# Seven VectorE operations for nine in the seven-product groups, and two more groups in that form

## The chip, the cores and the metric

The kernel runs on one core of one Trainium2 chip. The metric is device time in microseconds (us) of one execution of the whole program. TensorE does the matmuls, VectorE and ScalarE work on their results, SyncE (SP) issues nearly all transfers. In the rows PE is TensorE, PEld its weight loads, DVE is VectorE, ACT is ScalarE.

## What is computed

An attention over channels, then two feed-forward layers over 6016 tokens of 256 channels with 2048 hidden features each. The weights of the layers come as 64-bit floats and the kernel makes 32-bit ones of them.

```python
def _attn_ref(q, k, v, tau):
    qn = q / (np.linalg.norm(q, axis=1, keepdims=True) + 1e-06)
    kn = k / (np.linalg.norm(k, axis=1, keepdims=True) + 1e-06)
    s = kn.transpose(0, 2, 1) @ qn / tau
    a = softmax(s)                       # over the last axis
    return (v @ a).astype(np.float32)

def _moe_ref(x, w_in, w_out):
    r = np.maximum(x @ w_in, 0.0)
    return ((r * r) @ w_out).astype(np.float32)

def _moe2_ref(x, w_in, w_out):
    h = x @ w_in
    return (np.maximum(0.01 * h, h) @ w_out).astype(np.float32)
...
x = _attn_ref(**attn).reshape(6016, 256)
return _moe2_ref(_moe_ref(x, **moe), **moe2)
```

## The kernel before

**Tiling.** The tokens are cut into six pairs (p = 0 to 5) of two halves. A half has 512 tokens, in pair 4 it has 448. The hidden features are cut into eight groups (g = 0 to 7) of 256. One unit n is one layer, one pair and one group, so there are 96 units, and the last one is n = 95. In a unit the hidden values are a 2 x 2 block of quadrants: two blocks of 128 features (fb) by two halves of tokens.

**Precision.** Each operand is split into a high part, which ScalarE rounds (a cast), and a low part, which VectorE forms by subtracting the high part (`low`, line 109). A product is then three matmuls (`mm3`, line 540, matmul in line 543).

**First matrix product of a unit.** From unit 4 on it takes seven products F1 to F7 instead of eight: the weights w_in and the tokens are combined to sums and differences of quadrants first (`sums`, line 204; `prepare_x`), and the results accumulate in two banks, ha and hb (or hc and he). ScalarE and VectorE take them out into the tiles c, and ScalarE applies the nonlinear function.

**Second matrix product of a unit.** It has two forms. In the plain form ("P") there are eight products, and two double casts and two double low parts (of two quadrants, 1024 columns, each) prepare the operands. In the seven-product form ("S", the groups that the table GROUPS names) the products are P1 to P7. Their operands are quadrants and differences of quadrants, which VectorE forms in place; per unit that is nine operations of VectorE: a double low part G0, low part B22, the differences T1, T3, T2 and T4, a double low part G1, and the low parts T3 and T2. P2, P3, P4 and P7 accumulate in four y banks, P1 and P6 in the bank yA, P5 in yF. P6 of several units (a batch) is kept back and done together at the batch's end. VectorE empties yA into the sums P1 and U (`take_shared`, line 1672).

**The end of a pair.** `combine` adds the sums P1, U and V and the bank yF to the y banks; results are transposed on VectorE and stored.

**The end of the last pair.** The pair (2, 5) is mixed: groups 0 to 4 are in the seven-product form, the rest is plain. `BY_TOKENS` is the first group whose half 1 is done in another way (`second_by_tokens`, line 577): the tokens are the stationary operand, so that the result needs no transpose, in 24 matmuls of 256 columns per group into four banks (`by_token`). Before, these are groups 6 and 7. What the seven-product groups summed for half 1 must then join in: `combine_last` (line 1802) adds U, V and yF to the y banks on VectorE, transposes the two sums of half 1 into a tile o, and SP stores this tile to memory (`ys`, line 1834) and loads it back with the tokens in rows (`sums`, line 1841). `finish_last` (line 598) adds the four by-token banks to it and stores the result.

**The order.** A planner in the kernel (`build`, `simulate`) places tasks on the engines from costs and due times and writes each engine's list of instructions in that order. Each engine then takes its list strictly in turn and waits where an operand isn't there. On TensorE the first products F1 to F7 of a unit go in a fixed sequence, with second products of earlier units put between.

Of the kernel before, what the change touches and what calls it, by code (L numbers as in the profile page):

```python
# [19 lines left out]
P = 128  # L20
# [8 lines left out]
def attn_moe_moe2(  # L29
# [22 lines left out]
    GROUPS = {(1, 4): tuple(range(6)), (1, 5): tuple(range(6)), **{(2, p): tuple(range(7)) for p in range(5)}, (2, 5): tuple(range(5))}  # L52
# [43 lines left out]
    wi_d = {(L, g): dram.tile([P, 2, 8, P], F32, name=f"wi{L}_{g}") for L in (1, 2) for g in range(NG)}  # L96
# [27 lines left out]
    class Unit:  # L124
# [6 lines left out]
        def load(self):  # L131
# [6 lines left out]
            nc.sync.dma_start(t.rearrange("p a b w -> p a (b w)"), src)  # L138
# [29 lines left out]
        def into(self):  # L168

            if self.kind == "i" or self.blocks:  # L170
# [5 lines left out]
                return self.x, self.to[:, 0], self.to[:, 1]  # L176
# [21 lines left out]
        def store(self):  # L198
            if self.kind == "o":
                nc.sync.dma_start(wo_d[self.L, self.g], raw(self.to))  # L200
            elif self.L == 2:
                nc.sync.dma_start(wi_d[2, self.g][:, :, 1:], raw(self.to[:, :, 1:]))

    def sums(x, A11=1, A22=2, S1=4, S2=5, S3=6, S4=7):
# [8 lines left out]
    def out_sums(x):  # L213
        return sums(x, A11=2, A22=1, S1=5, S2=6, S3=7, S4=4)
# [355 lines left out]
    def second(n, half, fb, d):  # L570
# [3 lines left out]
        wo = both(wo_t[L, p, g], d, fb)  # L574
        mm3(y, wo, both(g_t[n, half], fb, slice(0, w)), begins((L, p, half, d)))

    def second_by_tokens(n, fb):
# [5 lines left out]
        for t in range(WIDTH[p] // P):  # L583
            if first:
                by_token.append(y_bank(L, p, 1, t) if t < KC else bank("ce"[t - KC], "y"))
            for m, (a, b) in enumerate(((0, 1), (0, 0), (1, 0))):
# [3 lines left out]
                    wo[:, b, :, fb],  # L590
# [44 lines left out]
    def shared(n, product, bank_key, first):  # L635
# [8 lines left out]
        else:  # L644
            a = both(late_w[n, "S2" if product == "P6" else "S3"], 0)
        x = {"P1": lambda: both(g_t[n, "G0"], 0, sl), "P2": lambda: both(g_t[n, "G0"], 1, sl),
             "P3": lambda: both(b_t[n, "B22"], sl), "P4": lambda: both(g_t[n, "G1"], 1, sl),
             "P5": lambda: both(g_t[n, "G1"], 0, sl), "P6": lambda: both(b_t[n, "T2"], sl),
             "P7": lambda: both(b_t[n, "T3"], sl)}[product]()
# [8 lines left out]

    def result(n, half, w, fb=None):
        c = c_t[n, half]  # L660
        return c[:, :, :w] if fb is None else c[:, fb, :w]
# [208 lines left out]
    KEEP = 8  # L870
    LATE_FIRST = True
# [9 lines left out]
    CONV_BEGIN, CONV_END = 1.4, 4  # L881
    N0 = 4
    FOLD_AFTER = "F1"
# [52 lines left out]
    A = {"A11": 1, "A22": 2, "A12": 3, "S1": 4, "S2": 5, "S3": 6, "S4": 7}  # L936
# [23 lines left out]
    FROM = {"P1": "G0", "P2": "G0", "P3": "B22", "P4": "G1", "P5": "G1", "P6": "T2", "P7": "T3"}  # L960
# [26 lines left out]
    def build(base):  # L987
# [33 lines left out]
        def convert(u, due, loaded=None, first=None, pace=4, begin=0):  # L1021
# [14 lines left out]
            if blocks:  # L1036
                raw_ = Buf("whl", 2, d(4))
                t = T("DVE", 3, d(4), u.high, deps=[t], alloc=raw_, uses=[w, cm])
                for i in range(4):
                    t = T("DVE", 1.1, d(4.2 + i / 10), lambda i=i: (sums if u.kind == "i" else out_sums)(u.x)[i](),  # L1040
                          deps=[t], uses=[raw_])
                to = Buf("wis", 1, d(5))
                t = T("ACT", 4.6, d(5), u.round, deps=[t], alloc=to, uses=[raw_])
                t = T("DVE", 5.2, d(6), u.low, deps=[t], uses=[raw_, to])
# [30 lines left out]
        def fold_sums(n, at_):  # L1075
# [19 lines left out]
            for i in range(4):  # L1095
                a = T("DVE", 1.1, at_ + 11 + i, lambda i=i: r["s"][i](), deps=[a], uses=[xb])
            h_ = T("ACT", 4.6, at_ + 16, lambda: nc.scalar.copy(wi_t[1, 0, g][:, 0], r["x"]), deps=[a], uses=[xb, b])
            lo = T("DVE", 5.2, at_ + 22, lambda: low(wi_t[1, 0, g][:, 1], r["x"], wi_t[1, 0, g][:, 0]), deps=[h_], uses=[xb, b])
            wi_ready[1, 0, g] = wi_ready[n + 1] = lo
            stores["i", 1, g, "s"] = T(  # L1100
                "SP", "wi", at_ + 30, lambda: nc.sync.dma_start(wi_d[1, g][:, :, 1:], raw(wi_t[1, 0, g][:, :, 1:])),
# [247 lines left out]
        def load_wi(n):  # L1349
            L, p, g = units[n]  # L1350
            b = wi_b[n] = Buf("wi", 3, base[n - 2] + 0.5)
            if n < 2 * NG and g < N0:
# [11 lines left out]
                def high():  # L1364
                    nc.scalar.copy(r["w"][:, 0, 4:], r["x"][:, 4:])
# [578 lines left out]
```

## Time and profile before

| | us |
|---|---|
| median of 3 runs | 1001.35 (1000.79 to 1002.28) |
| the profiled execution, its own time | 1002.93 |
| its span, first to last instruction | 1001.1 |
| TensorE busy | 994.6 |
| VectorE busy | 901.4 |
| ScalarE busy | 804.4 |

The granted TensorE clock is 1.000 over the whole span. Matmuls overlap in the records, so that a record is longer than the distance to the next one; the distance of starts tells what a matmul takes in a stream. The wait of a matmul for an operand shows as idle time of its weight load (PEld).

### The profile page before, as it was taken

How to read it: one execution, taken by the hardware profiler on the slowest of the kernel's cores; microseconds unless marked ns; L12 is line 12 of the kernel's file. 1: busy time of each engine (PE TensorE's matmuls, PEld its weight loads, DVE VectorE, ACT ScalarE, POOL GpSimd, SP SyncE). 2: the span in 40 equal slices, each digit the busy share in tenths (PEclk: the TensorE clock that was granted, in tenths of full speed). 3: DMA queues.
4: the chain of work that ended last, by engine and by line, in shares of the span. 5: the costliest groups of instructions: out<-in, count | busy, mean ns of one | idle time of the engine just before them, and what ended most of it. 6: DMA issues, size and time to landing. Idle time of an engine off the chain costs nothing.

```text
span 1001.1 us, 13148 instructions
## 1 busy us (share of the span) xinstructions
PE 994.6 (99%) x4528; PEld 837.3 (84%) x4528; DVE 901.4 (90%) x1314; ACT 804.4 (80%) x1184; POOL 0.7 (0%) x6
## 2 busy tenths in 40 slices
PE   9999999999999999999999999999999999999998
PEld 7888888887888888998888888888888888998887
DVE  4899999988988977999999999999999999998985
ACT  6799978877878777888898888779788788887773
POOL 0000000000000000000000000000000000000000
PEclk9999999999999999999999999999999999999999
DMA  9786559788978967965665665666577586676553
GB/s 339 281 253 205 200 193 287 266 308 296 332 284 294 318 249 265 316 219 206 223 209 200 229 215 202 201 217 226 172 219 233 182 239 227 210 233 220 195 143 84
DMA packets 160946, 234.97 MB, mean 235 GB/s; under 512 B 53232, under 2 KB 97264, under 8 KB 158576
## 3 DMA queue, kind: packets, MB, share of 16 engines
q1 hardware_dynamic: 160160, 233.48, 69.0%
q8 instruction: 36, 0.59, 0.2%
q10 hardware_dynamic: 720, 0.66, 0.2%
q14 instruction: 30, 0.25, 0.1%
HBM read 187.70 MB, written 46.40 MB: 234 GB/s over the span
## 4 chain that ended last, share of the span: by engine, by line
PE 97%; DMA 2%; DVE 0%; ACT 0%; ACTq 0%; issue 0%; SPq 0%
PE y L543 37%; PE ha L543 21%; PE hb L543 16%; PE yA L543 7%; PE yF L543 3%; PE hc L543 3%; PE sT L386 3%; PE he L543 2%; PE h L704 2%; PE pw L252 1%; DMA qk<-in_k_dram 1%; DMA qk<-in_q_dram 1%; PE y L587 0%; DVE o L552 0%; ACT e L472 0%; ACTq L338 0%
## 5 line engine op out<-in xcount | busy, mean ns | idle before, releaser
L543 PE MATMUL y<-g,wo 128*128 128x512 f32 (+1 forms) x1344 | 350.5, 387 | 0.0
L543 PEld LDWEIGHTS y<-g,wo 128*128 128x128 f32 x1344 | 252.1, 188 | 49.5 <-DVE wo L110 0.4
L543 PE MATMUL ha<-x,wi 128*128 128x512 f32 (+1 forms) x960 | 265.6, 385 | 0.0
L110 DVE TENSOR_TENSOR g<-c,g 128x1024 fp32r<-128x1024 f32 (+1 forms) x192 | 228.0, 1197 | 18.7 <-ACT g L674 13.9
L543 PEld LDWEIGHTS ha<-x,wi 128*128 128x128 f32 x960 | 180.0, 188 | 33.8 <-ACT c L1504 0.7
L543 PE MATMUL hb<-x,wi 128*128 128x512 f32 (+1 forms) x720 | 199.6, 386 | 0.1
L543 PEld LDWEIGHTS hb<-x,wi 128*128 128x128 f32 x720 | 134.3, 188 | 26.2 <-DVE c L550 1.7
L1612 DVE TENSOR_TENSOR c<-c 128x512 f32<-128x512 f32 (+1 forms) x208 | 139.9, 672 | 7.1 <-ACT c L691 1.2
L1587 ACT CAST g<-c 128x1024 fp32r<-128x1024 f32 (+1 forms) x104 | 105.2, 1023 | 5.1 <-PE y L543 2.4
L110 DVE TENSOR_TENSOR b<-c,b 128x512 fp32r<-128x512 f32 (+1 forms) x156 | 102.5, 668 | 2.0 <-ACT b L1605 1.7
L1605 ACT CAST b<-c 128x512 fp32r<-128x512 f32 (+1 forms) x156 | 93.1, 608 | 10.5 <-DVE c L1612 4.7
L681 ACT ACTIVATE c<-c 128x1024 f32<-128x1024 f32 (+1 forms) x96 | 100.0, 1043 | 1.5
L674 ACT CAST g<-c 128x1024 fp32r<-128x1024 f32 (+1 forms) x88 | 91.7, 1044 | 1.6
L1504 ACT COPY w<-ha 128x512 f32<-128x512 f32 (+1 forms) x80 | 46.2, 577 | 49.9 <-PE ha L543 49.6
L691 ACT ACTIVATE c<-c 128x512 f32<-128x512 f32 (+1 forms) x98 | 60.7, 621 | 8.8 <-DVE c L552 8.5
L1504 ACT COPY u<-ha 128x512 f32<-128x512 f32 (+1 forms) x80 | 46.0, 575 | 9.8 <-PE ha L543 6.9
L110 DVE TENSOR_TENSOR x<-xr,x 128x1024 fp32r<-128x1024 f32 (+3 forms) x47 | 49.1, 1051 | 0.6 <-ACT x L1261 0.6
L386 PE MATMUL sT<-qk 128*128 128x256 f32 x188 | 42.1, 382 | 1.4 <-DMA qk<-in_k_dram 1.3
L543 PE MATMUL yA<-g,wo 128*128 128x512 f32 (+1 forms) x156 | 42.9, 383 | 0.0
L543 PE MATMUL yF<-g,ws 128*128 128x512 f32 (+1 forms) x156 | 42.9, 383 | 0.0
L543 PE MATMUL y<-b,ws 128*128 128x512 f32 (+1 forms) x156 | 42.9, 383 | 0.0
L543 PE MATMUL y<-b,wo 128*128 128x512 f32 (+1 forms) x156 | 42.8, 383 | 0.0
(137 smaller groups left out, 1202.4 us busy)
## 6 DMA issues: line engine op xcount, KB each, us to landing
wi<-wi SPq DMA_DIRECT2D x88, 896.0 KB, 5.6
wo<-wo SPq DMA_DIRECT2D x84, 512.0 KB, 4.5
ws<-wo SPq DMA_DIRECT2D x120, 128.0 KB, 4.0
wst<-in_moe_w_in_dram SPq DMA_DIRECT2D x16, 512.0 KB, 6.0
wst<-in_moe_w_out_dram SPq DMA_DIRECT2D x16, 512.0 KB, 6.8
wi<-wis SPq DMA_DIRECT2D x8, 896.0 KB, 6.1
wo<-wis SPq DMA_DIRECT2D x7, 1024.0 KB, 7.6
wo<-wos SPq DMA_DIRECT2D x13, 512.0 KB, 5.8
```

The costliest lines, as they stand in the source:

```text
L110: tt(lo, x, raw(hi), op=ALU.subtract)
L252: nc.tensor.matmul(pw[:, i * 2 * P : (i + 1) * 2 * P], eT[:, a, j, i * P : (i + 1) * P], whl[g][:, b, j], start=t == 0 and (i == 0 or g == 0),
L386: nc.tensor.matmul(sT[j][:, :C], t[:, 0, i, j * P : (j + 1) * P], t[:, 1, i], start=n == 0 and i == 0, stop=last_tile and i == g - 1,)
L543: nc.tensor.matmul(ps, a[m], b[n], start=first and i == 0, stop=i == 2, skip_group_check=True)
L674: nc.scalar.copy(g_t[n, half][:, 0, :, :w], c)
L681: nc.scalar.activation(c, c, AF.Square)
L691: nc.scalar.activation(c, c, AF.Prelu, alpha=0.01)
L704: nc.tensor.matmul(h_t[n, half, fb][:, :w], a[i], b[j], start=start, stop=stop, skip_group_check=True)
L1504: nc.scalar.copy(to, h(0))
L1587: nc.scalar.copy(g_t[n, name][:, 0, :, :w], result(n, half, w))
L1605: nc.scalar.copy(b_t[n, name][:, 0, :w], c(half, fb))
L1612: tt(c(*to), c(*a), c(*b), op=ALU.subtract)
```

## The change

- **Seven operations for nine.** In seven-product units the tiles c hold a feature block's two halves together (by row) instead of a half's two feature blocks. The operands pair up in another way: GA is a row of results as it stands (for P2 and P3), GB is the other row after one difference T3 (for P1 and P7), GC is the first row with T2 subtracted from both quadrants in one operation (for P5 and P4), and T2 is a sum in a small tile of its own (t2, one buffer). VectorE has three double low parts, T3, T2, the double subtraction and one single low part. ScalarE has three double casts and a single one instead of two and three.
- **Two more groups.** Pair 5 of the first layer has seven groups in the form instead of six, pair 5 of the second layer has six instead of five. `BY_TOKENS` follows from that: it becomes 7, so that group 6 of the last pair is plain in both halves and only group 7 goes by tokens.
- **Weights.** The sum S4 is written over the quadrant A21, which isn't used any more, so that the tile wi has seven quadrants instead of eight and is stored and loaded in one piece. Two of the four operations on the sums become one double subtraction; for the second weights of the seven-product groups that asks for the two halves in turned places (`turned`), so each of these loads becomes two.
- **Planner.** The conversion of the second layer's weights may begin at 1.2 pairs instead of 1.4 (`CONV_BEGIN`), and the folding of the attention into the weights stands behind F2 instead of F1 (`FOLD_AFTER`). In a unit that doesn't end a batch, P1 stands behind P2 and P3.

```diff
-    GROUPS = {(1, 4): tuple(range(6)), (1, 5): tuple(range(6)), **{(2, p): tuple(range(7)) for p in range(5)}, (2, 5): tuple(range(5))}
+    GROUPS = {(1, 4): tuple(range(6)), (1, 5): tuple(range(7)), **{(2, p): tuple(range(7)) for p in range(5)}, (2, 5): tuple(range(6))}
     BY_TOKENS = max(GROUPS.get((2, 5), (-2,))) + 2
...
-        wi_t[key] = wpool.tile([P, 2, 8, P], F32R, tag="wi", name="wi", bufs=3)
+        wi_t[key] = wpool.tile([P, 2, 7, P], F32R, tag="wi", name="wi", bufs=3)
...
-            nc.sync.dma_start(t.rearrange("p a b w -> p a (b w)"), src)
+            to = t.rearrange("p a b w -> p a (b w)")
+            if turned(self.kind, self.L, g):
+                for b in range(2):
+                    nc.sync.dma_start(to[:, 1 - b], src[:, b])
+            else:
+                nc.sync.dma_start(to, src)
...
+        S2 = S3 + 1
         return [
             lambda: tt(x[:, S1], x[:, 0], x[:, A22], op=ALU.add),
-            lambda: tt(x[:, S3], x[:, A11], x[:, 0], op=ALU.subtract),
-            lambda: tt(x[:, S2], x[:, S1], x[:, A11], op=ALU.subtract),
+            lambda: tt(two(S3, S2), two(A11, S1), two(0, A11), op=ALU.subtract),
             lambda: tt(x[:, S4], x[:, 3], x[:, S2], op=ALU.subtract),
         ]
...
-    CONV_BEGIN, CONV_END = 1.4, 4
+    CONV_BEGIN, CONV_END = 1.2, 4
     N0 = 4
-    FOLD_AFTER = "F1"
+    FOLD_AFTER = "F2"
...
-    FROM = {"P1": "G0", "P2": "G0", "P3": "B22", "P4": "G1", "P5": "G1", "P6": "T2", "P7": "T3"}
+    FROM = {"P1": "GB", "P2": "GA", "P3": "GA", "P4": "GC", "P5": "GC", "P6": "T2", "P7": "GB"}
+    PART = {"P1": 0, "P2": 0, "P3": 1, "P4": 0, "P5": 1, "P7": 1}
...
-            t1 = T("DVE", 3 * s, t0 + 59, sub, (0, 0), (1, 0), (0, 0), deps=[n22, g0], uses=cb)
-            t3 = T("DVE", 3 * s, t0 + 61, sub, (1, 0), (1, 1), (1, 0), deps=[n12, t1], uses=cb[1:])
-            t2 = T("DVE", 3 * s, t0 + 65, sub, (1, 1), (1, 1), (0, 0), deps=[t3, b22], uses=cb)
-            t4 = T("DVE", 3 * s, t0 + 67, sub, (0, 1), (0, 1), (1, 1), deps=[t2], uses=cb)
...
+            def t3():
+                c = result(n, 1, w)
+                tt(c[:, 1], result(n, 0, w)[:, 1], c[:, 1], op=ALU.subtract)
+
+            def t2():
+                c = result(n, 1, w)
+                s_t[n, "t2"] = tpool.tile([P, 1, 512], F32, tag="t2", name="t2", bufs=T2_BUFS)
+                tt(s_t[n, "t2"][:, 0, :w], c[:, 0], c[:, 1], op=ALU.add)
+
+            def t4_t1():
+                c = result(n, 0, w)
+                tt(c, c, s_t[n, "t2"][:, :, :w].to_broadcast([P, 2, w]), op=ALU.subtract)
...
+            ca, cbb = cb[1], cb[0]
+            b = g_b[n, "GA"] = Buf("g", 4, t0 + 45)
+            t = T("ACT", A2, t0 + 45, pair_cast, "GA", 0, deps=[n22, n21], alloc=b, uses=[ca])
+            low_of[n, "GA"] = ga = T("DVE", D2, t0 + 52, pair_low, "GA", 0, deps=[t], uses=[b, ca])
+            d3 = T("DVE", 3 * s, t0 + 50, t3, deps=[n22, n12, n11], uses=cb)
+            b = g_b[n, "GB"] = Buf("g", 4, t0 + 52)
+            t = T("ACT", A2, t0 + 52, pair_cast, "GB", 1, deps=[d3], alloc=b, uses=[cbb])
+            low_of[n, "GB"] = gb = T("DVE", D2, t0 + 58, pair_low, "GB", 1, deps=[t], uses=[b, cbb])
+            t2b = Buf("t2", T2_BUFS, t0 + 53)
+            d2 = T("DVE", 3 * s, t0 + 53, t2, deps=[d3], alloc=t2b, uses=[cbb])
+            d41 = T("DVE", D2, t0 + 54, t4_t1, deps=[ga, d2], uses=[ca, t2b])
...
-                own = own if ends else [p1, *own]
+                own = own if ends else [*own, p1]
```

**How the order moves at the end of TensorE's list.** ha and hb are the last unit's first products, yA takes P1 and P6, yF takes P5, y stands for the four y banks and the by-token banks (the last row of each). These are the last twelve rows before the program's end. Before:

```order
L543 MATMUL yA<-b,ws 128x512 x3
L543 MATMUL y<-g,wo 128x512 x3
L543 MATMUL hb<-x_7811,wi 128x512 x3
L543 MATMUL ha<-x_7916,wi 128x512 x3
L543 MATMUL y<-g,wo 128x512 x3
L543 MATMUL hb<-x_7854,wi 128x512 x3
L543 MATMUL ha<-x_7854,wi 128x512 x3
L543 MATMUL y<-g,wo 128x512 x6
L543 MATMUL ha<-x_7916,wi 128x512 x3
L543 MATMUL hb<-x_7811,wi 128x512 x3
L543 MATMUL y<-g,wo 128x512 x33
L587 MATMUL y<-wo,g 128x256 x48
```

Now, in the changed program:

```order
L557 MATMUL ha<-x_7796,wi 128x512 x3
L557 MATMUL hb<-x_7775,wi 128x512 x3
L557 MATMUL y<-g,wo 128x512 x6
L557 MATMUL yA<-g,wo 128x512 x3
L557 MATMUL yF<-g,ws 128x512 x3
L557 MATMUL y<-g,wo 128x512 x3
L557 MATMUL y<-g,ws 128x512 x3
L557 MATMUL yA<-b,ws 128x512 x3
L557 MATMUL y<-g,wo 128x512 x3
L557 MATMUL yA<-b,ws 128x512 x6
L557 MATMUL y<-g,wo 128x512 x33
L601 MATMUL y<-wo,g 128x256 x24
```

The last product into yA (P6) stood ahead of six of the last unit's first products and 33 + 48 matmuls; now it stands behind all first products, with 33 + 24 matmuls behind it.

**How the order moves at the end of VectorE's list.** acc are the sums U and V of `combine_last`, o its transposed result (the first two transposes) and the results of half 0 and half 1 behind that, g a low part of the last units. Before, from the addition of the last yA on:

```order
L552 TENSOR_TENSOR acc<-acc,yA 128x512
L110 TENSOR_TENSOR g<-c,g 128x1024
L552 TENSOR_TENSOR acc<-acc 128x512
L552 TENSOR_TENSOR y<-y,acc 128x512
L552 TENSOR_TENSOR acc<-acc,yF 128x512
L552 TENSOR_TENSOR c<-w,hb 128x512
L552 TENSOR_TENSOR acc<-acc,y 128x512
L617 STREAM_TRANSPOSE o<-acc 128x16x32
L552 TENSOR_TENSOR acc<-acc,y 128x512
L617 STREAM_TRANSPOSE o<-acc 128x16x32
L552 TENSOR_TENSOR c<-u,hb 128x512
L110 TENSOR_TENSOR g<-c,g 128x1024 x2
```

Now, from the same addition on:

```order
L566 TENSOR_TENSOR acc<-acc,yA 128x512
L110 TENSOR_TENSOR g<-c,g 128x1024
L566 TENSOR_TENSOR acc<-acc 128x512
L566 TENSOR_TENSOR acc<-acc,yF 128x512
L566 TENSOR_TENSOR y<-y,acc 128x512
L566 TENSOR_TENSOR acc<-acc,y 128x512
L631 STREAM_TRANSPOSE o<-acc 128x16x32
L566 TENSOR_TENSOR acc<-acc,y 128x512
L631 STREAM_TRANSPOSE o<-acc 128x16x32
L631 STREAM_TRANSPOSE o<-y 128x16x32 x2
L566 TENSOR_TENSOR o<-y,sums 128x256 x4
```

The additions and transposes follow each other with one low part among them; the last unit's own work (c, g) used to stand between and behind them and now stands ahead, but for that one low part.

## Rows read from the trace of the kernel before

**Rows 1.** The page, parts 1 and 4: busy us (share) xinstructions; chain by engine

```profile
PE 994.6 (99%) x4528; PEld 837.3 (84%) x4528; DVE 901.4 (90%) x1314; ACT 804.4 (80%) x1184; POOL 0.7 (0%) x6
PE 97%; DMA 2%; DVE 0%; ACT 0%; ACTq 0%; issue 0%; SPq 0%
```

**Rows 2.** Timeline of PE at the end: start us, us, operation, count

```profile
976.76 0.84 PE L543 MATMUL yA<-b,ws 128*128 128x512 f32 x3
...
984.24 7.64 PE L543 MATMUL y<-g,wo 128*128 128x512 f32 x33
991.72 5.91 PE L587 MATMUL y<-wo,g 128*128 128x256 f32 x48
```

**Rows 3.** Timeline of DVE at the end: start us, us, operation [idle before]

```profile
978.63 1.23 DVE L110 TENSOR_TENSOR g<-c,g 128x1024 fp32r<-128x1024 f32 x1 [0.17 <-ACT g L674]
979.77 0.69 DVE L552 TENSOR_TENSOR acc<-acc 128x512 f32<-128x512 f32 x1
980.50 0.70 DVE L552 TENSOR_TENSOR y<-y,acc 128x512 f32<-128x512 f32 x1
981.10 0.68 DVE L552 TENSOR_TENSOR acc<-acc,yF 128x512 f32<-128x512 f32 x1
...
982.95 0.68 DVE L552 TENSOR_TENSOR acc<-acc,y 128x512 f32<-128x512 f32 x1
983.66 0.71 DVE L617 STREAM_TRANSPOSE o<-acc 128x512 f32<-128x512 f32 x1
984.30 0.65 DVE L552 TENSOR_TENSOR acc<-acc,y 128x512 f32<-128x512 f32 x1
984.98 0.71 DVE L617 STREAM_TRANSPOSE o<-acc 128x512 f32<-128x512 f32 x1
...
991.92 1.31 DVE L617 STREAM_TRANSPOSE o<-y 128x512 f32<-128x512 f32 x2 [2.65 <-PE y L543]
996.60 1.50 DVE L552 TENSOR_TENSOR o<-y,sums 128x256 f32<-128x256 f32 x4 [3.36 <-PE y L587]
```

**Rows 4.** Waits of PEld over the span: us in total, times, longest us

```profile
PEld hb L543 <- DVE c L550: 1.7, 5, 0.5
...
PEld y L543 <- DVE wo L110: 0.4, 1, 0.4
...
PEld hb L543 <- ACT hb L1504: 0.2, 1, 0.2
```

**Rows 5.** Timeline of SP at the end: start us, us of issue, transfer

```profile
985.72 2.00 SPq L1834 DMA_DIRECT2D ys<-o  x4
989.58 0.38 SPq L1841 DMA_DIRECT2D sums<-ys  x1
```

**Rows 6.** DMA issues from 980 us on: count, KB each, median us to landing

```profile
out_dram<-o SPq DMA_DIRECT2D x5, 128.0 KB, 3.4
ys<-o SPq DMA_DIRECT2D x4, 128.0 KB, 2.2
sums<-ys SPq DMA_DIRECT2D x1, 512.0 KB, 3.8
```

**Rows 7.** Groups by line: form xcount, busy us, mean ns of one, idle before

```profile
L110 DVE TENSOR_TENSOR g<-c,g 128x1024 fp32r<-128x1024 f32 (+1 forms) x192 | 228.0, 1197 | 18.7 <-ACT g L674 13.9 <-ACT g L1587 3.0
L1612 DVE TENSOR_TENSOR c<-c 128x512 f32<-128x512 f32 (+1 forms) x208 | 139.9, 672 | 7.1 <-ACT c L691 1.2
...
L232 DVE STREAM_TRANSPOSE xr<-v 128x512 f32<-128x512 f32 (+1 forms) x20 | 13.6, 687 | 0.5 <-DMA v<-in_v_dram 0.5
...
L1270 DVE TENSOR_TENSOR xr<-xr 128x1024 f32<-128x1024 f32 (+1 forms) x11 | 13.2, 1197 | 0.8 <-DMA xr<-x 0.7
```

**Rows 8.** Timeline at 242 us: a transpose of v, then the late weight load

```profile
242.06 0.71 DVE L232 STREAM_TRANSPOSE xr<-v 128x512 f32<-128x512 f32 x1 [0.48 <-DMA v<-in_v_dram]
243.40 0.53 PEld L543 LDWEIGHTS hb<-x,wi 128*128 128x128 f32 x3 [0.49 <-DVE c L550]
```

**Rows 9.** Busy us by stretch, 250 to 420 us: engines, PEclk, DMA share, GB/s

```profile
250.00:420.00 170.00, 170.00 (x761) 142.00 (x760) 144.80 (x228) 134.04 (x179) 0.00 (x0) 1.00 0.83 294
```

More of the change, by code (lines that the diff above doesn't have):

```diff
@@ L175, in into @@
                     self.to = cpool.tile([P, 2, 8, P], F32R, tag="wis", name="wis", bufs=1)
-                return self.x, self.to[:, 0], self.to[:, 1]
+                k = 7 if self.L == 2 and self.kind == "i" else None
+                return self.x[:, :k], self.to[:, 0, :k], self.to[:, 1, :k]
             if self.L == 1:
@@ L213, in out_sums, with turned @@
     def out_sums(x):
-        return sums(x, A11=2, A22=1, S1=5, S2=6, S3=7, S4=4)
+        return sums(x, A11=2, A22=1, S1=5, S3=6, S4=4)
+    SUM_TIMES = 1.1, 1.8, 1.1
+    def turned(kind, L, g):
+        return kind == "o" and g in SG[L]
     v_t = {}
@@ L573, in second @@
         y = y_bank(L, p, half, d)[:, :w]
-        wo = both(wo_t[L, p, g], d, fb)
+        wo = both(wo_t[L, p, g], d, 1 - fb if turned("o", L, g) else fb)
         mm3(y, wo, both(g_t[n, half], fb, slice(0, w)), begins((L, p, half, d)))
@@ L645, in shared @@
             a = both(late_w[n, "S2" if product == "P6" else "S3"], 0)
[L646 to L649, printed above, removed]
+        x = both(b_t[n], sl) if product == "P6" else both(g_t[n, FROM[product]], PART[product], sl)
         if bank_key[0] == "y":
@@ L657, in shared, with by_fb @@
         mm3(y[:, :w], a, x, first)
+    def by_fb(n):
+        return is_mixed(*units[n][:2]) and form_of(n) == "S"
     def result(n, half, w, fb=None):
-        c = c_t[n, half]
-        return c[:, :, :w] if fb is None else c[:, fb, :w]
+        if fb is None:
+            return c_t[n, half][:, :, :w]
+        if by_fb(n):
+            half, fb = fb, half
+        return c_t[n, half][:, fb, :w]
     def new_result(n, half):
@@ L1038, in convert @@
                 t = T("DVE", 3, d(4), u.high, deps=[t], alloc=raw_, uses=[w, cm])
-                for i in range(4):
-                    t = T("DVE", 1.1, d(4.2 + i / 10), lambda i=i: (sums if u.kind == "i" else out_sums)(u.x)[i](),
+                for i in range(3):
+                    t = T("DVE", SUM_TIMES[i], d(4.2 + i / 10), lambda i=i: (sums if u.kind == "i" else out_sums)(u.x)[i](),
                           deps=[t], uses=[raw_])
                 to = Buf("wis", 1, d(5))
-                t = T("ACT", 4.6, d(5), u.round, deps=[t], alloc=to, uses=[raw_])
-                t = T("DVE", 5.2, d(6), u.low, deps=[t], uses=[raw_, to])
+                t = T("ACT", 4.1 if u.kind == "i" else 4.6, d(5), u.round, deps=[t], alloc=to, uses=[raw_])
+                t = T("DVE", 4.7 if u.kind == "i" else 5.2, d(6), u.low, deps=[t], uses=[raw_, to])
             else:
@@ L1412, in wo_sums @@
             t = T("DVE", 3, e, join, deps=[ready], alloc=xb, uses=[b])
[L1413 to L1414 removed]
+            for i in range(3):
+                t = T("DVE", SUM_TIMES[i], e + 1, lambda i=i: r["s"][i](), deps=[t], uses=[xb])
             wb = Buf("wis", 1, e + 6)
@@ L1531, in unit @@
             f = {}
+            cq = (lambda half, fb: cb[1 - fb]) if by else (lambda half, fb: cb[half])
             def F_(name, deps):
```

127 lines of the change are left out of this document (58 added, 69 removed).

## The prediction

> **What bounds the kernel now.** I read the page first, then the waits of the weight loads, then the last 25 us of the timeline engine by engine. On the page TensorE is busy 99% of the span, and the chain that ended last is 97% TensorE [rows 1]. So a time comes from two things: how many matmuls stand in TensorE's stream, and what keeps the stream from running on or the end from following it.
>
> The price of one matmul is read where nothing waits: the 33 that begin at 984.24 are followed at 991.72, so one of 512 columns takes 7.48 / 33 = 0.2267 us. Of the 48 short ones of 256 columns behind them, 39 have to end until the first of four banks is complete. VectorE's addition of that bank starts at 996.60, and it starts 0.20 us behind TensorE (991.92 against 991.72). So a short one takes (996.60 - 991.72 - 0.20) / 39 = 0.120 us [rows 2, 3].
>
> How much waiting is in the stream? Eight groups of waiting weight loads, from 1.7 down to 0.2 us, sum to 4.1 us from the first feed-forward layer on. VectorE ends four of these, 1.7, 0.4, 0.4 and 0.2, 2.7 us in all [rows 4]. TensorE is full, and nothing but 4.1 us can be won there without taking matmuls out.
>
> The page's other figure seems to say something else: weight loads are busy only 84% of the span [rows 1]. A weight load takes 837.3 / 4528 = 0.185 us on the mean, and where nothing waits there is one in every 0.2267 us, 82% [rows 1, 2]. So 84% is what a full stream looks like here, not 16% of idle time.
> The Trainium skill, in Perfetto Trace Analysis, Identifying the Most-Contended Engine, says the contrary of matmul busy time: it is no measure of the distance to the roofline, and the busy share of LDWEIGHTS is. Read as room for waits to be closed, its 16% would be 160 us that a lighter VectorE could bring nearer; by the rows it can bring 4.1 us at most, and I take the rows.
>
> Then the end. The sums of the last pair's seven-product groups go out to memory and come back in another layout: VectorE adds them up and transposes them, SP stores them (ys) and loads them (sums), and the final four additions need them. Today these additions wait for TensorE: they begin at 996.60 and the row names the short matmuls as what released them [rows 3]. The sums had been there since 989.58 + 3.8 = 993.4 [rows 5, 6]. So today the round trip is hidden, with 3.2 us to spare.
>
> **Matmuls removed.** Two more groups take the seven-product form, one in pair 5 of each layer. Each saves one product of three matmuls, six in all. By the order of the changed program 12 matmuls of 512 columns (half 1 of the group with number 6) come in the place of 24 short ones. Together that is 12 - 6 = 6 more long and 24 fewer short: 6 x 0.2267 - 24 x 0.120 = -1.5 us. All of it lies on TensorE, on the path. Left alone it gives 1001.35 - 1.5 = 999.8.
>
> **VectorE and ScalarE.** A seven-product group had two double subtractions for the low part (1.20 us), four quadrant subtractions and three single low parts of half that size (0.67): 2 x 1.197 + 7 x 0.672 = 7.10 us. Now it has three double low parts, one double subtraction with a repeated operand, one quadrant subtraction, one addition and one single low part. The trace has no double operation with a repeated operand; the nearest row is a plain double subtraction of float32, 1.197 us, and the bounds are 0.67 (as a single one) and 1.34 us (as two). I take 1.20, since the work per element is the same: 4 x 1.197 + 3 x 0.672 = 6.80 us [rows 7]. With 52 groups that is -16 us; the two groups that change form cost 2 x (6.80 - 2 x 1.197) = +9 us; three operations instead of four in the weight sums save some 3 us. VectorE loses about 10 us of 901. ScalarE casts the same seven quadrants in four operations instead of five and loses a few us. Both lie beside TensorE. What of it reaches the end is bounded by the 2.7 us that VectorE makes TensorE wait. I take nothing: the changed program orders every engine anew, so these small waits are drawn again. Loads and stores of the first weights become one piece in a row instead of two, which TensorE doesn't wait for now. The second weights come in two loads of half the size; SP issues 7 such pairs for each layer, 14 issues more, and behind them stand the loads of v (rivals).
>
> **The end.** Here the change is dear. The round trip starts when the last P6 product is in the bank yA; VectorE's `acc<-acc,yA` is first in its chain. Before, this product ends at 976.76 + 3 x 0.2267 = 977.44 and stands ahead of six of the last unit's seven first products [rows 2]. Afterwards it stands behind all of them: by the order only 33 long and 24 short matmuls follow. Two sums decide, both counted from the end of that product.
>
> What the round trip needs afterwards. VectorE starts 0.20 us behind TensorE, as above. Then in the order's sequence, by distances of starts in the trace: the add into U 0.60 (an operation that the next one doesn't depend on: 980.50 to 981.10), the double low part 1.14 (978.63 to 979.77), V + U 0.73 (979.77 to 980.50), the add of yF 0.60, the add into y 0.70, then add, transpose, add, transpose 0.71 + 0.64 + 0.68 + 0.71 (982.95 to 985.69), and 0.03 to SP [rows 3, 5]. That is 6.7 us. From the first store's issue at 985.72 to the landing of sums at 993.4 it is 7.7 us [rows 5, 6]. Together 14.4 us.
>
> What covers it. Before: 991.72 - 977.44 = 14.3 us of long matmuls and products, and 4.9 us of short ones until the first of the four banks is complete (996.60) [rows 2, 3], 19.2 us against the 16 us that the trip then took. After: 33 x 0.2267 = 7.5 us, and 15 of 24 short ones, 15 x 0.120 + 0.2 = 2.0 us. That is 9.5 us.
>
> So the additions wait 14.4 - 9.5 = 4.9 us for the sums, where they wait for TensorE now. Behind them everything stays as it is (996.60 to the end). Net: -1.5 + 4.9 = +3.4 us.
>
> The store and the load are prices from the trace. The out stores of half 0 stand behind the load on SP and would then fly together with it; before, they were issued at its landing. Their landing took 3.4 us against 2.2 us for ys [rows 6], so the load may land 0 to 1.2 us later; I take 0, since its packets are ahead in the queue.
> The Trainium skill, DMA: Bandwidth & Descriptors, Anatomy of one DMA, gives a fit for transfers that GpSimd issues, 2.0 us and one more for every 436 KB. An estimate by it for a store of 128 KB and a load of 512 KB is 2.3 and 3.2 us, and the two of the trip would then be some 0.5 us shorter than measured, an end of 1004.2; SP's transfers here are slower, and the rows decide.
>
> **Sum.** 1001.35 + 3.4 = 1004.7 us. The profiled execution took 1002.93 us with a span of 1001.1; the span should come to 1004.5, and an execution like it to 1006.3. The median of the three runs is 1001.35, lower by 1.6 us than the profiled one, and the forecast is put on the median.
>
> **Rivals.** First, the waits close. VectorE is lighter by 10 us, its low parts come sooner, and the 2.7 us that it makes TensorE wait go. Then 1004.7 - 2.7 = 1002.0, not slower by what can be measured; with ScalarE's part too 1000.6. It decides from about 1.4 us won. For it: 1.7 of the 2.7 us lie at the additions into c, short operations that a shorter queue lets through sooner [rows 4]. Against it: they come from VectorE's place in its queue, and the queue is ordered anew, not merely thinned.
>
> Second, new waits in the first layer. The second layer's weights are converted from 1.2 pairs on instead of 1.4, so that their loads meet those of v sooner, and SP issues more. In the trace VectorE waited once, 0.48 us at a transpose for v, and an addition behind it was late for TensorE by as much [rows 8]; it is the one wait of 20 such transposes [rows 7], and DMA is 83% busy in 250 to 420 us [rows 9]. If half of the 20 meet that, it is 10 x 0.5 = 5 us, and the time 1009.7. For it: the load on DMA. Against it: one of 20 waits now.
>
> Third, the trip stays hidden, and the change gives what its matmuls say: 999.8, within what counts as the same. It needs 4.9 us that I can't find in the order. That the form isn't applied can be left out: the order shows the six matmuls gone.
>
> **How the numbers follow.** 0.2% is 2.0 us, about what a measurement of this kernel can tell from no change. The forecast gets 0.72, closed waits 0.11, new waits 0.11, a hidden trip 0.06. Slower by over 2.0 us (over 1003.35) is nearly all of the forecast and all of the new waits: 0.80. The same takes most of the closed waits and of the hidden trip: 0.15. Faster (under 999.35) needs both of these together: 0.05. The range goes from 1002.0 (VectorE's waits gone) to 1008.0: 1.2 for the shared flight of the load and about 2 us of new waits above the forecast.
>
> **What would show it.** Right: the four additions at the end are released by the DMA sums<-ys and not by TensorE, some 7 us behind the first short matmul; TensorE's last matmul lies 1.5 us earlier than before; a matmul still takes 0.227 us. VectorE's busy time should fall by about 10 us, and a double subtraction with a repeated operand should take 1.2. Wrong: the additions released by TensorE at 2 us behind the first short matmul (third rival), or waits of weight loads that sum to over 6 us (second) or under 2 us (first).

## The result and the profile after

| | before | changed |
|---|---|---|
| median (6 runs each) | 1001.75 us (1000.79 to 1002.28) | 1009.47 us (1007.57 to 1010.93) |
| profiled execution, its own time | 1002.93 | 1008.42 |
| its span | 1001.1 | 1006.6 |

The changed kernel is slower: ratio 1.0077, 95% interval 1.0061 to 1.0092, or 7.7 us by the medians. The forecast was 1004.7 with a range up to 1008.0. Its direction was right, its size too small.

Parts 1 and 4 of the page of the changed kernel, which answer to [rows 1] (busy us, share, number of instructions; then the chain that ended last, by engine):

```profile
PE 993.5 (99%) x4510; PEld 835.7 (83%) x4510; DVE 898.9 (89%) x1200; ACT 797.9 (79%) x1141; POOL 0.7 (0%) x6
PE 96%; DMA 2%; DVE 1%; ACT 0%; issue 0%; SPq 0%; DVEq 0%
```

Eighteen matmuls are gone, as meant. VectorE has 114 instructions fewer, but its busy time fell by only 2.5 us.

The end of the changed kernel. First TensorE's timeline (start us, us, operation), which answers to [rows 2]:

```profile
984.95 1.52 PE L557 MATMUL yA<-b,ws 128*128 128x512 f32 x6
986.31 7.72 PE L557 MATMUL y<-g,wo 128*128 128x512 f32 x33
993.87 3.03 PE L601 MATMUL y<-wo,g 128*128 128x256 f32 x24
```

VectorE's timeline in the same stretch, with the idle time before in brackets ([rows 3] of before):

```profile
986.51 0.69 DVE L566 TENSOR_TENSOR acc<-acc,yA 128x512 f32<-128x512 f32 x1 [0.60 <-PE yA L557]
987.11 1.22 DVE L110 TENSOR_TENSOR g<-c,g 128x1024 fp32r<-128x1024 f32 x1
988.25 0.69 DVE L566 TENSOR_TENSOR acc<-acc 128x512 f32<-128x512 f32 x1
...
992.41 0.71 DVE L631 STREAM_TRANSPOSE o<-acc 128x512 f32<-128x512 f32 x1
994.07 1.31 DVE L631 STREAM_TRANSPOSE o<-y 128x512 f32<-128x512 f32 x2 [0.95 <-PE y L557]
1001.96 1.41 DVE L566 TENSOR_TENSOR o<-y,sums 128x256 f32<-128x256 f32 x4 [6.58 <-DMA sums<-ys]
```

SP's issues there ([rows 5] of before):

```profile
993.15 2.09 SPq L1861 DMA_DIRECT2D ys<-o  x4
997.59 0.38 SPq L1868 DMA_DIRECT2D sums<-ys  x1
998.07 2.64 SPq L641 DMA_DIRECT2D out_dram<-o  x4
```

The DMA issues from 980 us on (count, KB each, median us to landing; [rows 6] of before):

```profile
out_dram<-o SPq DMA_DIRECT2D x5, 128.0 KB, 4.1
ys<-o SPq DMA_DIRECT2D x4, 128.0 KB, 2.5
sums<-ys SPq DMA_DIRECT2D x1, 512.0 KB, 4.2
```

The four additions at the end were released by TensorE before. Now they wait 6.58 us, and the row names the load of the sums. They start 1001.96 - 993.87 = 8.1 us behind the first short matmul. By TensorE alone it would be 2.0 us, so 6.1 us of waiting are new.

There is a second new place, at 541 us, which the prediction doesn't have. The issue of a load on SP, then ScalarE's and TensorE's timeline there:

```profile
533.20 0.54 SPq L1263 DMA_DIRECT2D xr<-x  x1
...
540.00 0.62 ACT L1280 CAST x<-xr 128x512 fp32r<-128x512 f32 x1 [1.39 <-DMA xr<-x]
540.53 1.05 ACT L1612 CAST g<-c 128x1024 fp32r<-128x1024 f32 x1
541.48 0.62 ACT L708 ACTIVATE c<-c 128x512 f32<-128x512 f32 x1
542.01 0.57 ACT L1526 COPY hb<-ha 128x512 f32<-128x512 f32 x1
...
540.54 1.52 PE L557 MATMUL yA<-b,ws 128*128 128x512 f32 x6
542.64 0.96 PE L557 MATMUL hb<-x,wi 128*128 128x512 f32 x3 [0.58 <-ACT hb L1526]
```

xr<-x is the load of the next pair's tokens of the second layer. ScalarE waits for it 1.39 us with a cast. Three operations behind that cast in its queue is the copy hb<-ha, and TensorE's next first product waits for the copy. Nothing but the order of the queue ties the copy to the load. In the kernel before, ScalarE's queue had the two in the other order, and the cast didn't wait:

```profile
542.65 0.58 ACT L1504 COPY hb<-ha 128x512 f32<-128x512 f32 x1
543.16 1.56 ACT L1261 CAST x<-xr 128x512 fp32r<-128x512 f32 x2
```

### The profile page after: what moved, and what is told of

Read it like the earlier page. It is cut to its first block, busy times and chain, and to the rows that moved or that the text cites. A ratio compares the mean times of both kernels' runs of the same rounds, so it can differ in the third digit from the quotient of the medians.

```text
span 1006.6 us, 12966 instructions
## 1 busy us (share of the span) xinstructions
PE 993.5 (99%) x4510; PEld 835.7 (83%) x4510; DVE 898.9 (89%) x1200; ACT 797.9 (79%) x1141; POOL 0.7 (0%) x6
## 4 chain that ended last, share of the span: by engine, by line
PE 96%; DMA 2%; DVE 1%; ACT 0%; issue 0%; SPq 0%; DVEq 0%
PE y L557 36%; PE ha L557 21%; PE hb L557 16%; PE yA L557 7%; PE yF L557 4%; PE sT L400 4%; PE hc L557 3%; PE he L557 2%; PE h L721 2%; PE pw L266 1%; DMA qk<-in_k_dram 1%; DMA xr<-x 1%; DMA sums<-ys 0%; DVE acc L566 0%; DMA ys<-o 0%
## 5 line engine op out<-in xcount | busy, mean ns | idle before, releaser
L557 PE MATMUL y<-g,wo 128*128 128x512 f32 (+1 forms) x1482 | 386.7, 387 | 0.0
L557 PEld LDWEIGHTS y<-g,wo 128*128 128x128 f32 x1482 | 278.0, 188 | 54.0 <-DVE y L566 0.2
L110 DVE TENSOR_TENSOR g<-c,g 128x1024 fp32r<-128x1024 f32 (+1 forms) x246 | 292.0, 1194 | 22.5 <-ACT g L691 12.3
L1612 ACT CAST g<-c 128x1024 fp32r<-128x1024 f32 (+1 forms) x162 | 165.2, 1026 | 11.5 <-PE y L557 4.0
L691 ACT CAST g<-c 128x1024 fp32r<-128x1024 f32 (+1 forms) x84 | 87.7, 1044 | 2.9 <-PE y L557 0.9
L1629 DVE TENSOR_TENSOR c<-c,t 128x1024 f32<-128x1024 f32 (+1 forms) x54 | 64.3, 1190 | 1.4
L557 PE MATMUL y<-g,ws 128*128 128x512 f32 (+1 forms) x162 | 44.7, 384 | 0.0
L1280 ACT CAST x<-xr 128x1024 fp32r<-128x1024 f32 (+3 forms) x44 | 40.2, 925 | 3.4 <-DMA xr<-x 1.6
L566 DVE TENSOR_TENSOR c<-u,hb 128x512 f32<-128x512 f32 (+1 forms) x48 | 32.3, 673 | 11.5 <-PE hb L557 11.5
L557 PE MATMUL yA<-b,ws 128*128 128x512 f32 (+1 forms) x162 | 42.4, 384 | 0.0
```

Source lines behind the costliest of these rows:

```text
L110: tt(lo, x, raw(hi), op=ALU.subtract)
L557: nc.tensor.matmul(ps, a[m], b[n], start=first and i == 0, stop=i == 2, skip_group_check=True)
L566: tt(to, a, b, op=ALU.add)
L691: nc.scalar.copy(g_t[n, half][:, 0, :, :w], c)
L1280: nc.scalar.copy(part(0), src())
L1612: nc.scalar.copy(g_t[n, name][:, 0, :, :w], result(n, i, w))
```

## The experiments

The medians of before in the three sets of runs were 1001.33 (25 runs), 1001.37 (21) and 1001.20 (7). The ratios below are against the runs beside them.

**1. The changed kernel without the trip through memory.** The last addition takes the transposed sums as they lie, so that half 1 of the last pair is added up in a wrong layout. TensorE's order is that of the changed kernel.

```diff
-        sums = last_sums["t"].rearrange("p t (q k c) -> p t q k c", q=Q, k=KC)
+        last = o_t[last_sums["key"]].rearrange("p g c -> p (g c)").rearrange("p (t c) -> p t c", c=C)
+        sums = last.rearrange("p t (q k c) -> p t q k c", q=Q, k=KC)
...
-            t = T("SP", "out", t0 + 60, keep, deps=ts_, uses=[o], lat=LOAD)
-            b = o_b[L, p, "back"] = Buf("v", 3, t0 + 61)
...
-            done[L, p, 1, "all"] = [T("SP", "wo", t0 + 61, load, deps=[t], alloc=b)]
+            last_sums["key"] = key
+            done[L, p, 1, "all"] = list(ts_)
```

> The changed kernel without the store and the load of the last pair's sums: the final four additions take the transposed tile o as it lies on chip. Left out is that the sums come back with the tokens in rows, so that half 1 of the last pair is added in the wrong layout. TensorE's order is the same, matmul by matmul. Theory (the round trip is exposed): the additions are released by TensorE again, some 2 us behind the first short matmul where the changed kernel has 8.1, and the time falls by 6.1 us to about 1003.4, with its runs as close together as those of the kernel before. Rival (the loss lies in the stream or in the stores behind the additions): under 2 us fall, over 1007.5.

Measured 1003.2 us (8 runs, 1002.04 to 1006.32), ratio 1.0024 (1.0013 to 1.0036). The end of its timelines, TensorE and VectorE:

```profile
993.39 3.03 PE L601 MATMUL y<-wo,g 128*128 128x256 f32 x24
...
995.38 1.50 DVE L566 TENSOR_TENSOR o<-y,o 128x256 f32<-128x256 f32 x4 [0.48 <-PE y L601]
```

The additions start 2.0 us behind the first short matmul again, as the prediction counted from 15 short ones. The median is 6.3 us under that of the changed kernel (5.3 us by the two ratios), and the trace had 6.1 us of waiting. So the trip is the larger part of the loss. The runs don't lie as close together as expected: they spread over 4.3 us, those of the kernel before over 3.0. The stop at 541 us is in this trace too, with 0.60 us.

**2. Five groups in the last pair, as before; all else of the change stays.**

```diff
-(2, 5): tuple(range(6))}
+(2, 5): tuple(range(5))}
```

> The changed kernel with five groups of the last pair in the seven-product form, as before, and seven in pair 5 of the first layer. Theory (the sixth group of the last pair alone exposes the round trip): the load of the sums lands before the short matmuls need it, the additions wait for TensorE; one product less than before is -0.7 us, and the slower matmuls of 448 columns seen in the changed kernel (206.7 for 202.7 ns in the seven-product sweeps) are +1.6: about 1002.7. Rival (the seven operations or the new order cost the time): about 1009.

Measured 1003.66 us (12 runs, 1001.04 to 1005.62), ratio 1.0021 (1.0012 to 1.0031), a miss upwards. The trip was hidden: the additions were released by TensorE, as in [rows 3]. The 1.6 us that were expected of slower 448-column matmuls are not in this trace (248 of them in 860 to 910 us, see number 8). The rest lay at 541 us. The load, ScalarE's cast and TensorE there, and the additions at the end:

```profile
532.28 0.54 SPq L1263 DMA_DIRECT2D xr<-x  x1
...
540.46 0.62 ACT L1280 CAST x<-xr 128x512 fp32r<-128x512 f32 x1 [2.76 <-DMA xr<-x]
...
539.62 1.52 PE L557 MATMUL yA<-b,ws 128*128 128x512 f32 x6
543.09 1.11 PE L557 MATMUL hb<-x,wi 128*128 128x512 f32 x3 [1.95 <-ACT hb L1526]
544.00 1.48 PE L557 MATMUL ha<-x,wi 128*128 128x512 f32 x3
545.28 1.48 PE L557 MATMUL y<-g,wo 128*128 128x512 f32 x3
546.56 1.15 PE L557 MATMUL hb<-x,wi 128*128 128x512 f32 x3
...
998.68 1.50 DVE L566 TENSOR_TENSOR o<-y,sums 128x256 f32<-128x256 f32 x4 [3.36 <-PE y L601]
```

A stretch of it by the view of windows (us, then the busy time of PE, PEld, DVE, ACT and POOL, then PEclk, DMA share and GB/s):

```profile
544.00:546.00 2.00, 2.00 (x6) 1.61 (x5) 1.97 (x3) 1.10 (x3) 0.00 (x0) 0.50 0.36 103
```

This is the stop of the changed kernel, grown, since the load landed 8.2 us after its issue (in the changed kernel 6.8): TensorE is idle for 1.95 us, and then the granted clock is 0.50, its level of 1.2 GHz. Three matmuls take 545.28 - 544.00 = 1.28 us instead of 0.68. By the distances of starts the stop and the slow stretch together are some 3.9 us in this execution, which took 1005.1 us.

**3. The groups of before, all else of the change stays.** This is the new VectorE form with its weights and the planner's numbers, without the new groups.

```diff
-(1, 5): tuple(range(7)), ..., (2, 5): tuple(range(6))}
+(1, 5): tuple(range(6)), ..., (2, 5): tuple(range(5))}
```

> The changed kernel with the groups of the kernel before in both layers, so that only the seven operations, the weights in seven quadrants and the planner's numbers differ. Theory: no product less, the round trip hidden, 448 columns at 206.7 ns: 1001.75 + 1.6 = 1003.3. First rival (a lighter VectorE closes waits): under 1000. Second rival (the new operand pairs and the order cost time by themselves): over 1006.

Measured 1002.72 us (11 runs, 1001.21 to 1003.49), ratio 1.0011 (1.0002 to 1.0019). Part 1 of its page:

```profile
PE 992.6 (99%) x4528; PEld 838.1 (84%) x4528; DVE 887.7 (89%) x1185; ACT 793.3 (79%) x1136; POOL 0.7 (0%) x6
```

VectorE is 901.4 - 887.7 = 13.7 us lighter, and the time doesn't fall. It is rather 1.1 us (by the ratio) to 1.4 us (by the medians) longer. Where that comes from is not shown: the profiled execution was the fastest of the eleven, and its 448-column matmuls were not slow, against the 1.6 us in the expectation. So seven operations for nine buy nothing by themselves. The first rival, that a lighter VectorE closes waits of the weight loads, has no support.

The stop at 541 us isn't there either. The load xr<-x goes out 8 us earlier than in the changed kernel, and the cast finds it landed:

```profile
524.78 0.33 SPq L1263 DMA_DIRECT2D xr<-x  x1
534.47 0.65 ACT L1280 CAST x<-xr 128x512 fp32r<-128x512 f32 x1
```

**4. The kernel before with a sixth group in the last pair.** Its VectorE form and weights are those of before.

```diff
-(2, 5): tuple(range(5))}
+(2, 5): tuple(range(6))}
```

> The kernel before, nine operations, with six groups of the last pair in the seven-product form instead of five. Theory: TensorE -0.8 us (one product, and short matmuls replaced), and the round trip as exposed as in the changed kernel, +6.1: about 1007.0, the additions released by the load of the sums. Rival (the exposure needs the new order of VectorE): the additions wait for TensorE and the time is 1001.

Measured 1007.29 us (5 runs, 1006.67 to 1008.65), ratio 1.0062 (1.0050 to 1.0074). The end of TensorE, VectorE and SP:

```profile
992.69 3.03 PE L587 MATMUL y<-wo,g 128*128 128x256 f32 x24
...
1000.94 1.42 DVE L552 TENSOR_TENSOR o<-y,sums 128x256 f32<-128x256 f32 x4 [6.74 <-DMA sums<-ys]
...
992.64 2.02 SPq L1834 DMA_DIRECT2D ys<-o  x4
```

The wait is 6.74 us although nothing else of the change is there. One group more in the last pair opens the trip in either form of VectorE's work, and costs 6.0 us by the medians, with the 0.8 us that TensorE was expected to save already in it.

**5. and 6. A later landing for xr<-x in the planner.** The planner is told to count on a landing 9 units of its time later, so that it puts the operations on xr further back. Number 5 has five groups in the last pair (number 2 with this), number 6 is the changed kernel with this.

```diff
                 self.moves = kb / RATE[piece]
+                self.late = 9 if cost == "x" else 0
...
-                x.lat = max(moved, x.end) + LANDS - x.end
+                x.lat = max(moved, x.end) + LANDS + x.late - x.end
```

> The changed kernel with five groups of the last pair as before (its round trip is hidden), and with the planner's landing time of the loads xr<-x (a pair's activations, 1 MB) put 9 of its units, some 2 us, later, so that what reads them stands further back on ScalarE and VectorE. Second theory (beside the round trip): in the changed order ScalarE stands at a cast of xr while the load lands 1 to 3 us late, the copy hb behind it is late, TensorE stops for 0.7 to 2 us and then runs at half clock for a while; this makes the scatter and 1 to 4 us. Then the time falls from 1003.7 to about 1001.0, with runs within 2 us of each other. Rival (the scatter is of the chip or of the 448-column matmuls): no change, 1003.7, runs 4 us apart.

> The changed kernel, all its groups, with the same later landing time for the loads xr<-x. Theory: the round trip stays exposed (additions released by the load of the sums, 8 us behind the first short matmul), the stop at 541 us goes: from 1009.5 to about 1007.2. Rival: 1009.5.

Number 5 took 1001.89 us (11 runs, 1000.74 to 1002.97), ratio 1.0004 (0.9995 to 1.0013), 1.8 us under number 2 (1.7 by the ratios, whose intervals touch). Number 6 took 1006.63 us (5 runs, 1006.16 to 1007.29), ratio 1.0047 (1.0035 to 1.0060), 2.8 us under the changed kernel (3.0 by the ratios). Both came within 0.9 us of what was expected. ScalarE's cast at this place and VectorE's additions at the end, in number 6:

```profile
547.72 0.62 ACT L1281 CAST x<-xr 128x512 fp32r<-128x512 f32 x1
...
1000.83 1.42 DVE L566 TENSOR_TENSOR o<-y,sums 128x256 f32<-128x256 f32 x4 [6.63 <-DMA sums<-ys]
```

The cast no longer waits, and the trip stands open as before. The edit also moves other operations, so 2.8 us is the price of the late load together with what else was drawn again. The intervals of the changed kernel and of number 6 just don't meet (1.0061 and 1.0060).

**7. The kernel before with seven groups in pair 5 of the first layer.** The other half of the new groups, alone.

```diff
-(1, 5): tuple(range(6))
+(1, 5): tuple(range(7))
```

> The kernel before, nine operations, with seven groups instead of six in pair 5 of the first layer. Theory: one product less and no new wait, since ScalarE and VectorE read xr later in its order than in the changed kernel: 1001.3 - 0.7 = 1000.6. Rival (the seventh group itself makes the load of x late, whatever the operations): a wait for xr at the start of the second layer, and 1002 to 1005.

Measured 1001.61 us (11 runs, 1000.97 to 1002.99), ratio 1.0000 (0.9992 to 1.0009). The product that it saves isn't seen. What was expected of it, 0.7 us, lies inside the interval, so this neither shows nor refutes it. VectorE's busy time rose from 901.4 to 908.5 us. The load xr<-x goes out as late here as in the changed kernel, at 534.01 us, but TensorE doesn't stop. The copy stands ahead of the cast, and in this execution the load landed sooner, 5.1 us after its issue:

```profile
539.86 0.57 ACT L1504 COPY hb<-ha 128x512 f32<-128x512 f32 x1 [0.35 <-PE ha L543]
...
541.54 0.61 ACT L1261 CAST x<-xr 128x512 fp32r<-128x512 f32 x1
```

With numbers 2 and 3 this places the stop: neither the new form alone nor the seventh group alone has it in its trace; the two together have it in all four traces without the edit of numbers 5 and 6 (the changed kernel, numbers 1, 2 and 8).

**8. The changed kernel once more,** without an edit, for what differs between executions of one program.

> The changed kernel once more, for a second profile of it. Theory: the two parts that move from run to run are the stop of TensorE at about 541 us behind the load xr<-x (0.7 us in the first profile) and the spacing of the 448-column matmuls (202.7 or 206.7 ns in each of the two 448-column seven-product sweeps); a run 2 us longer than the first has the longer stop. Rival: both are as in the first profile and the difference lies elsewhere, for example in the round trip.

It took 1008.77 us. The load, ScalarE's cast and TensorE at 541 us:

```profile
532.70 0.54 SPq L1263 DMA_DIRECT2D xr<-x  x1
...
540.81 0.62 ACT L1280 CAST x<-xr 128x512 fp32r<-128x512 f32 x1 [2.69 <-DMA xr<-x]
...
543.44 0.96 PE L557 MATMUL hb<-x,wi 128*128 128x512 f32 x3 [1.88 <-ACT hb L1526]
```

The window from 860 to 910 us, with matmuls of 448 columns, in this execution (columns as above):

```profile
860.00:910.00 50.00, 50.00 (x248) 46.20 (x247) 45.35 (x60) 39.75 (x67) 0.00 (x0) 1.00 0.73 225
```

The same window in the first profile of the changed kernel:

```profile
860.00:910.00 50.00, 50.00 (x243) 45.30 (x242) 44.50 (x59) 38.96 (x66) 0.00 (x0) 1.00 0.71 220
```

The stop is 1.88 us here and was 0.58 in the first profile, because xr<-x landed 8.1 us after its issue instead of 6.8. The same program loses different times at this place. The whole is only 0.35 us longer than in the first profile; the 448-column matmuls took 1.7 us less in this execution.

**9. Number 6, and the four stores of half 0 behind everything else.** Nothing flies beside the load of the sums.

```diff
+    by_token_done = []
...
         nc.sync.dma_start(to[:, 3:], o[1][:, 1:])
+        by_token_done.append(1)
+        put((2, 5, 0))
...
+        if key == (2, 5, 0) and not by_token_done:
+            return
```

> The changed kernel with the later landing of xr<-x, as e6, and one thing more: the four stores of the last pair's half 0 (out) are issued behind everything else instead of right behind the load of sums, so that nothing flies together with that load. In e6 the load was issued at 996.23 and landed 4.47 us later; in the kernel before and in the kernel with five groups, where no store follows at once, it took 3.79 and 3.87. Theory (the stores behind it slow the load): it lands within 3.9 us again, and the additions start 0.6 us earlier against the first short matmul (8.15 us in e6, 7.55 here). Rival (the load is slow because it reads memory that was written a moment ago, or for another reason): it stays at 4.2 to 4.5 us. The end itself comes later than in e6 under both, since four stores are issued behind the last one: by about 1.5 us, 1008 us.

It took 1009.32 us (one run), 1.3 us more than expected. Its DMA issues from 980 us on:

```profile
ys<-o SPq DMA_DIRECT2D x4, 128.0 KB, 2.3
sums<-ys SPq DMA_DIRECT2D x1, 512.0 KB, 3.8
```

The load takes 3.85 us (996.68 to 1000.52) against 4.47 in number 6. So the stores behind it do slow it, by about 0.6 us. The other traces agree: where stores follow the load at once (the changed kernel, numbers 4, 6, 8 and 10) it takes 4.2 to 4.5 us, where none does (the kernel before, numbers 2, 3, 5, 7 and 9) 3.8 to 3.9. The additions start 7.88 us behind the first short matmul, not 7.55, because the stores of the sums were late in this run: they landed 4.5 us after their first issue, in number 6 4.1. What makes the stores' time differ, this run doesn't show.

**10. Number 6, and two of the four stores of the sums issued by ScalarE.**

```diff
-                    nc.sync.dma_start(to, o_t[key][b * 32 : (b + 1) * 32])
+                    (nc.sync if b < 2 else nc.scalar).dma_start(to, o_t[key][b * 32 : (b + 1) * 32])
```

> The changed kernel with the later landing of xr<-x, as e6, and one thing more: of the four stores of the sums (ys) two are issued by ScalarE, which has nothing left to do, and two by SyncE. Theory (the end waits for the round trip, link after link): the issue takes 1.0 us instead of 2.1, the last store lands 1.0 us earlier, and so do the load, the additions and the end: 1006.6 - 1.0 = 1005.6 us. Rival (the stores share a limit beyond the queue's issue, or ScalarE is late): the last store lands when it did, 1006.6.

Measured 1007.45 us (4 runs, 1005.98 to 1008.48), ratio 1.0055 (1.0038 to 1.0072), no gain on number 6, and 1.9 us more than expected. Its DMA issues:

```profile
ys<-o SPq DMA_DIRECT2D x2, 128.0 KB, 2.4
ys<-o ACTq DMA_DIRECT2D x2, 128.0 KB, 3.0
```

All four are issued within 0.93 us, but the last one lands 4.04 us after the first issue (4.12 in number 6). What was saved in issuing comes back in flight, and the rival holds. The Trainium skill, DMA: Bandwidth & Descriptors, Issuing engines are not separate DMA queues, says that transfers of several issuing engines share the same DMA engines and that only issue time is saved. The trace agrees, and here not even that reached the landing.

None of these kernels is faster than the kernel before. Numbers 5 and 7 are level with it.

## Why the prediction came out too low

The parts are: TensorE -1.5 (as counted from the matmuls), the trip +6.1 (the wait in the trace), the late load and what came with it +2.8 (the medians of the changed kernel and number 6), in sum +7.4 us of the 7.7 measured. The forecast was +3.4. Of the 4.3 us that it lacked, 1.2 are the trip's price and 2.8 are waits in the new order, which it put at nothing; 0.3 stay open. That the trip would be exposed was right, and numbers 1 and 4 show it, by taking the trip out and by opening it alone. The +2.8 is less firm, since the edit of number 6 moves other operations too: the stop itself cost some 0.7 us in the first profile and 2.0 in number 8.

**The two matmul prices held.** The 33 long ones took 993.87 - 986.31 = 7.56 us, 0.08 more than 33 x 0.2267, with a small wait at 990 us among them. 24 short ones and 15 of them to the first additions gave the 2.0 us of experiment 1. "TensorE's last matmul 1.5 us earlier" did not show. It ended at 996.90 instead of 997.63, 0.7 us earlier. In that execution the 448-column matmuls took 1.6 us more (below) and the stop at 541 us some 0.7; against them, the profiled execution of before had lost some 1.5 us by its first 448-column matmul, which starts at 383.46, in the changed kernel at 382.01. The seventh group comes only behind that point, and number 7, in the old form, begins there at 381.94. So most of these 1.5 us are of the execution and not of the change.

**The cover held, the trip was dearer.** One step that failed is the price of the trip. VectorE's part was counted as 6.7 us and took 993.15 - 986.31 = 6.84. From the first store's issue to the landing of the sums it was taken as 7.7, from [rows 5, 6], and took 1001.83 - 993.15 = 8.7. From the landing to the first addition another 0.13 us passed, which the prediction didn't count. The wait is therefore 6.1 and not 4.9. Two links grew:

- the load, from 3.8 to 4.2 us (4.47 in number 6). The prediction had this as "0 to 1.2 us later; I take 0, since its packets are ahead in the queue". Number 9 shows that the reason doesn't hold: with the stores out of the way it is 3.85.
- the stores, from 3.7 us (first issue to last landing) to 4.3 (4.0 to 4.5 in numbers 6, 8 and 9). In the changed form SP paused some 0.35 us before one of the four issues. It did so in all four traces of this form in which SP issues the four stores with six groups in the last pair, and not in number 4 (3.75 us). What holds SP there is open.

The Trainium skill's fit, which the prediction weighed (DMA: Bandwidth & Descriptors, Anatomy of one DMA), would have made the trip 0.5 us shorter. The traces go the other way, up to 1 us longer than before.

**"I take nothing" for the new order.** This step failed too, and cost the forecast more. The prediction saw that all queues are ordered anew and gave new waits a chance of 0.11, but at the loads of v in the first layer, where none came. The place that broke is another, and its row stood among the prediction's own: the last line of [rows 7] shows VectorE's L1270 waiting 0.7 us for xr<-x in the kernel before. It was read for the duration of a double subtraction and not for its wait. In the changed order ScalarE's cast stands at that edge as well, with the copy for TensorE behind it; it takes the new form and the seventh group together (numbers 2, 3 and 7). The waits of VectorE and ScalarE for this load in the changed kernel (us in total, times, longest):

```profile
DVE xr L1289 <- DMA xr<-x: 1.9, 4, 0.6
ACT x L1280 <- DMA xr<-x: 1.6, 2, 1.4
```

**VectorE: -10 predicted, -2.5 measured.** The new operations cost what was taken. The groups by line of the changed kernel (count, busy us, mean ns):

```profile
L110 DVE TENSOR_TENSOR g<-c,g 128x1024 fp32r<-128x1024 f32 (+1 forms) x246 | 292.0, 1194 | 22.5 <-ACT g L691 12.3 <-ACT g L1612 9.0
L1629 DVE TENSOR_TENSOR c<-c,t 128x1024 f32<-128x1024 f32 (+1 forms) x54 | 64.3, 1190 | 1.4
```

The double subtraction with a repeated operand was taken as 1.20 us and took 1.190. The form with its weights made VectorE 13.7 us lighter (number 3) where the prediction's terms sum to 16 + 3 = 19, and the two groups cost 898.9 - 887.7 = 11.2 us and not 9. A part of the error is in adding up durations. Records of a full queue overlap: the addition at 986.51 is 0.69 us long and the next operation begins 0.60 behind it, the double low part at 987.11 is 1.22 long and the next begins 1.14 behind it. By such distances a unit goes from 2 x 1.14 + 7 x 0.60 = 6.48 to 4 x 1.14 + 3 x 0.60 = 6.36 us, a gain of 0.12 and not 0.30. The measured gain lies between the two sums, and I didn't follow it further, since it changed nothing of the time.

**The rivals.** Closed waits: no (number 3). A hidden trip: no, it is the main loss. New waits: right in kind, wrong in place, and it came on top of the forecast, not instead of it. That its time of 1009.7 us lies beside the measured 1009.5 is chance: its 5 us were waits for v. Its sign, over 6 us of waiting weight loads, came to 3.8 us in the first profile, counted as the prediction did, and to 6.6 in number 8. The range ended at 1008.0 because it took the load's 1.2 us and 2 us of new waits as a limit. In the two profiles of the changed kernel the stop cost 0.7 and 2.0 us, in number 2, with a slow stretch behind it, 3.9.

## What to carry to other kernels

When work is taken from the end of a kernel, list what still covers each transfer there and count from the last operand to the landing; price the transfers as they will run after the change, with the traffic that will then fly beside them. When a planner draws an order anew, look first for loads whose consumers already wait a few tenths in the trace, and read what stands behind those consumers in their queues. A lighter engine that isn't the bound bought nothing here, and adding up durations made it look lighter than it became.

## What was not expected of the hardware

- **A short stop can cost twice.** TensorE idle for 1.95 us was followed by a stretch at granted clock 0.50 (number 2). After 1.88 us (number 8) and 0.58 us the clock stayed at 1.00. Why it fell in one and not in the other, these runs don't show.
- **One program, two spacings.** The 681 matmuls of 448 columns took 140.0 us in the first profile of the changed kernel and 138.3 in number 8, with the same granted clock: 243 against 248 of them in 860 to 910 us. Before, it was 138.4. They lie in two stretches, pair 4 of each layer; numbers 1, 7 and 10 have the wider spacing in one of the two, so it is not of the new form (number 7 has the old one). What decides it is open; it moves this kernel by up to 1.7 us between executions.
- **The landing of one load varies.** xr<-x (1 MB) landed 5.1 to 8.9 us after its issue in two executions of the changed kernel, by place. At 541 us it was 6.8 and 8.1, with a DMA share of 0.99 and 0.97 from 535 to 540 us.
